# Single scores of two key tiles copied by VectorE, and one exponential for both

## The chip, the cores and the metric

The kernel runs on one core of a Trainium2 chip. A core has engines that work side by side, each through its own queue of instructions in order: TensorE (PE, with its weight loads shown as PEld), VectorE (DVE), ScalarE (ACT), GpSimd (POOL), and SyncE (SP), which issues most DMAs. They meet through semaphores: an instruction can wait for a count that another engine raises. Matrix products are written to PSUM, eight banks of 128 partitions x 512 single-precision numbers; the other engines read them there.

The metric is the device time of one execution, in microseconds (us).

## The reference

The input x is 2048 rows of 448 numbers. Two kinds of layer alternate, attention and feed-forward, twice, with the same weights both times:

```
x = x + A(layernorm(x)); x = x + B(layernorm(x)); x = x + A(layernorm(x)); x = x + B(layernorm(x))

A: q = (x wq) in 16 heads of 28;  k = x wk, v = x wv  (one head of keys and values, shared)
   p = softmax(q k^T * 28**-0.5);  o = p v;  result = o wo
B: (silu(x w_gate) * (x w_up)) w_down        with 1792 hidden columns
```

All is single precision.

## The kernel before

**Precision.** Most products are made of three reduced-precision ones (high x high, low x high, high x low), so a score tile takes three rounds of matmuls, z = 0, 1, 2 in `step` (line 604).

**Scores.** Queries are cut into 16 groups: 4 chunks of 512 queries by 4 groups of 4 heads. For each group the 16 key tiles of 128 keys are gone through. `step(n)` makes the scores of one key tile for four heads: 4 matmuls of 32 rows a round, side by side on PE. Three heads go to a triple of PSUM banks (`three`, there are two, in turn), the fourth head, the single score (`one`), to bank 6 or 7. Two key tiles, an even and an odd step, make a pair. There are 128 pairs in a layer, 256 in the kernel.

**Exponentials.** ACT makes the exponential of the triple in one instruction of 1,536 elements a partition (line 617 in an even step, 611 in an odd one) into `pt`, which has three buffers. In an even step ACT makes the single score's exponential first, straight from PSUM (line 616). In an odd step DVE copies the single score to SBUF (`raw`, line 613), and ACT makes its exponential from there, after the triple's (line 614).

**Value product.** After an odd step, `pv(d - 1)` multiplies the probabilities of the pair before with the values (line 647): 8 matmuls, four of the even tile and four of the odd one. Values have a column of ones, so the row sums come with the product. It is written to the bank that held the even single score of the current pair, and accumulated by DVE in SBUF (line 657; line 654 copies it for the first pair of a group).

The banks of the singles change hands in this order: value product of pair d − 1 and even single score of pair d + 1 use one of banks 6 and 7 and its neighbour by turns, given by `single`. On PE the order of a pair is: even scores, odd scores, value product of the pair before.

**Around it.** When a group is finished, `post` loads its row sums (SP, line 668), and three pairs later the block in `due` runs: two checks and a reciprocal on DVE (lines 674 to 676), a store and a reload on SP (678, 679), a product and a split in high and low part on POOL (686, 139, 140). In `scores` this block comes at the end of an odd step, behind `pv` and `between`. `between` issues, once in four groups, the output projection of a finished chunk (line 587), 48 matmuls, whose results DVE adds to x (591). Pieces of the next normalisation are put behind single steps through `later` (statistics, scaling, transposes, and lines 283 and 288, which make high and low part of the transposed input). After step 1 of a layer, `maxima` (line 424 on PE, 426 to 435 on DVE) makes row maxima of the last chunk, with bank 6 for its product.

The order on each engine is as the program writes it down; nothing is rearranged (a manual schedule).

Of the kernel before, what the change touches and what calls it, by code (L numbers as in the profile page):

```python
# [8 lines left out]
F32 = mybir.dt.float32  # L9
F32R = mybir.dt.float32r  # L10
AF = mybir.ActivationFunctionType
# [4 lines left out]
P = 128  # L16
# [11 lines left out]
SCALE = DH ** -0.5  # L28
# [24 lines left out]
def forward(  # L53
# [14 lines left out]
    nc = tc.nc  # L68
# [88 lines left out]
    def weights(fc):  # L157
        fs = slice(P * fc, P * fc + P)
        r = wpool.tile([P, 4, 2, P], F32, name="wr")
        for b, src in enumerate((w_gate, w_up)):  # L160
            rows3(r[:, :, b, :], src[:, fs])
        rd = wpool.tile([P, D], F32, name="wdr")
        nc.sync.dma_start(rd, w_down[fs, :])
        h = wpool.tile([P, 4, 2, P], F32R, name="wgh", bufs=FG + 1)
        l = wpool.tile([P, 4, 2, P], F32R, name="wgl", bufs=FG + 1)
        dh = wpool.tile([P, D], F32R, name="wdh", bufs=FG + 1)
        dl = wpool.tile([P, D], F32R, name="wdl", bufs=FG + 1)
        split(h, l, r)
        split(dh, dl, rd)
        return h, l, dh, dl  # L170
# [161 lines left out]
    class Attention:  # L332
# [232 lines left out]
        def scores(self, ff):  # L565
            next(switch)
            with tc.tile_pool(name=f"at{self.layer}", bufs=1, reuse_waits="tile") as wp:
                woh = wp.tile([P, NG, D], F32R, name="woh")
                wol = wp.tile([P, NG, D], F32R, name="wol")
                on, accs, pts = {}, {}, {}  # L570
                todo, due = [], {}
                single = lambda d: banks[6 + d % 2]

                def load_wo(z):
                    r = wpool.tile([P, 4, 2, P], F32, name="wr").rearrange("p (z k) b n -> p z (k b n)", z=2)
                    nc.gpsimd.memset(r, 0.0)
                    for j in range(4):
                        nc.sync.dma_start(r[32 * j : 32 * j + DH, :, 0:D], wos[j][:, 2 * z : 2 * z + 2, :])
                    zs = slice(2 * z, 2 * z + 2)
                    split(woh[:, zs, :], wol[:, zs, :], r[:, :, 0:D])  # L580
# [14 lines left out]
                def step(n):  # L595


                    i, kt = divmod(n, NT)
                    three, one = threes[n % 2], single(n // 2 + n)
                    q, k, ks = qts[i % 2], keys[kt // 4], slice(P * (kt % 4), P * (kt % 4) + P)  # L600
                    for z, (kp, part) in enumerate(((0, 0), (1, 0), (0, 1))):
                        for j in range(4):
                            js = slice(32 * j, 32 * j + 32)
                            nc.tensor.matmul(  # L604
                                three[:, j, :] if j < 3 else one, k[js, kp, ks], q[js, part, :],
                                start=(z == 0), stop=(z == 2), tile_position=(32 * j, 0),
                            )
                    pt = wp.tile([P, 3, 512], F32, name="pt", bufs=3)
                    pt1 = wp.tile([P, 512], F32, name="pt1", bufs=3)
                    if n % 2:  # L610
                        nc.scalar.activation(pt, three, AF.Exp, scale=SCALE)  # L611
                        raw = wp.tile([P, 512], F32, name="raw")
                        nc.vector.tensor_copy(raw, one)  # L613
                        nc.scalar.activation(pt1, raw, AF.Exp, scale=SCALE)  # L614
                    else:
                        nc.scalar.activation(pt1, one, AF.Exp, scale=SCALE)  # L616
                        nc.scalar.activation(pt, three, AF.Exp, scale=SCALE)  # L617
                    pts[n] = [*(pt[:, j, :] for j in range(3)), pt1]

                def between(d):  # L620

                    i, kt = divmod(2 * d, NT)
                    free, one = threes[0], single(d + 1)
                    if full:
                        self.lent = free[:, 0, :]
                        if 6 <= kt < 14:
                            self.advance(min(NM // 4, NM * (i + 2) - self.done))
                        if kt == 14 and i + 1 < len(GR):
                            self.places[i + 1](free[:, 1, :])
                    if not todo or kt != 10:  # L630
                        return
                    c = todo.pop()
                    adds = []
                    for t in (1, 2, 3):
                        adds.append(outproj(c, t, free[:, t - 1, :]))
                    for f in adds:
                        f()
                    outproj(c, 0, one)()

                def pv(d):  # L640


                    i, kt = divmod(2 * d, NT)
                    po = single(d + 1)
                    for n in (2 * d, 2 * d + 1):
                        for j in range(4):
                            nc.tensor.matmul(  # L647
                                po[32 * j : 32 * j + 32, :], vsb[:, n % NT, :], pts[n][j],
                                start=(n == 2 * d), stop=(n > 2 * d), skip_group_check=True,
                            )  # L650
                        del pts[n]
                    if kt == 0:
                        accs[i] = halves("o2").bitcast(F32)
                        nc.vector.tensor_copy(by_tile(accs[i][:, 0, :]), in_turn(po))
                    else:
                        acc = by_tile(accs[i][:, 0, :])
                        nc.vector.tensor_tensor(acc, in_turn(po), acc, ALU.add)  # L657
                    if kt == NT - 2:
                        due[d + 3] = post(i)
# [34 lines left out]
                for c in range(3):  # L694
                    ff.X[c] = xtile(xpool) if c < 2 else None
                    fs, got = norm_steps(c, True)
                    n = NT * (4 * c + 5)
# [10 lines left out]
                for n in range(last):  # L708
                    i, kt = divmod(n, NT)
                    if kt == 0 and i + 1 < len(GR):  # L710
                        self.parts(i + 1)
                    if kt == 3 and i + 1 < len(GR) and not full:
                        self.rows(i + 1)
                    if kt == 12 and i + 2 < len(GR):
                        self.stack(i + 2)
                    if i in (2, 3) and kt == 8:
                        load_wo(i - 2)
                    if n == NT and ff.nxt:
                        ff.nxt.below(nc.sync)
                    if kt == 8 and 10 < i <= 11 + FG:  # L720
                        ff.W[i - 11] = weights(i - 11)
                    step(n)
                    if not full and n == 1:
                        self.maxima(NC - 1, (6,))
                    if n in later:
                        later.pop(n)()
                    d, odd = divmod(n, 2)
                    if odd:
                        if d:
                            pv(d - 1)  # L730
                        between(d)
                        if d in due:
                            due.pop(d)()
                pv(last // 2 - 1)
                self.lent = None
                next(switch)
# [251 lines left out]
    for c in range(1, NC):  # L988
        fs, got = norm_steps(c)
        n = 4 * c - 4  # L990
# [38 lines left out]
```

## Time and profile before

| | |
|---|---|
| median of 3 runs | 1986.07 us (1986.04 to 1986.16) |
| span of the profiled execution | 1984.8 us |
| PE busy | 1969.2 us, 99% |
| ACT busy | 1278.6 us, 64% |
| DVE busy | 812.1 us, 41% |
| POOL busy | 528.7 us, 27% |
| granted PE clock | full in all slices but those at the very end, 0.98 from 1900 us on |

The profile is of one execution; the page gives its span, from the first instruction to the last, and no other time of it. Rows of groups read: line, engine, operation, output <- input, shapes, count | busy time in all, mean duration in ns of one | idle time of the engine just before them, with what ended it. Rows of the timeline read: start (us from the span's start), duration, engine, line, operation, output <- input, and in brackets the idle time ahead of it and what ended it. Successive instructions of one engine can overlap a little, so the distance of two starts can be less than the duration. In attention, roughly 64 to 572 us and 1046 to 1555 us of the span, ACT is busiest; in feed-forward PE.

### The profile page before, as it was taken

How to read it: one execution, taken by the hardware profiler on the slowest of the kernel's cores; microseconds unless marked ns; L12 is line 12 of the kernel's file. 1: busy time of each engine (PE TensorE's matmuls, PEld its weight loads, DVE VectorE, ACT ScalarE, POOL GpSimd, SP SyncE). 2: the span in 40 equal slices, each digit the busy share in tenths (PEclk: the TensorE clock that was granted, in tenths of full speed). 3: DMA queues.
4: the chain of work that ended last, by engine and by line, in shares of the span. 5: the costliest groups of instructions: out<-in, count | busy, mean ns of one | idle time of the engine just before them, and what ended most of it. 6: DMA issues, size and time to landing. Idle time of an engine off the chain costs nothing. (4 is left out here: it accounts for less than half of the span.)

```text
span 1984.8 us, 44687 instructions
## 1 busy us (share of the span) xinstructions
PE 1969.2 (99%) x18519; PEld 1322.9 (67%) x18519; DVE 812.1 (41%) x1410; ACT 1278.6 (64%) x2140; POOL 528.7 (27%) x571
## 2 busy tenths in 40 slices
PE   9999999999999999999999999999999999999998
PEld 7544545445458999999984444454454789988887
DVE  7444543544434222322554335445454432222222
ACT  4899797997953333333349998979979433333332
POOL 4212111132213233333341221111231232233320
PEclk9999999999999999999999999999999999999999
DMA  5101020121210011100131111102111101011102
GB/s 163 55 23 31 23 51 21 32 58 28 72 33 9 24 32 32 32 24 19 51 107 35 30 31 30 44 12 61 32 55 45 31 17 30 18 31 32 32 1 76
DMA packets 93382, 77.52 MB, mean 39 GB/s; under 512 B 23510, under 2 KB 76374, under 8 KB 93174
## 3 DMA queue, kind: packets, MB, share of 16 engines
q1 hardware_dynamic: 92886, 74.16, 13.5%
q8 instruction: 146, 2.39, 0.5%
q14 instruction: 62, 0.51, 0.1%
q10 hardware_dynamic: 288, 0.46, 0.1%
HBM read 55.06 MB, written 18.74 MB: 37 GB/s over the span
## 5 line engine op out<-in xcount | busy, mean ns | idle before, releaser
L647 PE MATMUL bank<-pt,vsb 128*32 128x512 f32 x4096 | 493.3, 598 | 0.5
L604 PE MATMUL bank<-qstack,keys 32*128 32x512 f32 x1536 | 484.2, 424 | 1.7 <-DVE xres L591 1.7
L604 PE MATMUL three<-qstack,keys 32*128 32x512 f32 x4608 | 461.4, 425 | 1.5 <-DVE vt L538 1.2
L604 PEld LDWEIGHTS three<-qstack,keys 32*128 32x128 f32 x4608 | 254.2, 182 | 295.0 <-ACT pt L617 181.1
L321 PE MATMUL bank<-xh,wgh 64*128 64x512 f32 x1728 | 437.5, 389 | 0.1
L611 ACT ACTIVATE pt<-three 128x1536 f32<-128x1536 f32 x256 | 372.2, 1454 | 0.6 <-ACT pt L617 0.3
L617 ACT ACTIVATE pt<-three 128x1536 f32<-128x1536 f32 x256 | 372.0, 1453 | 0.0
L321 PE MATMUL bank<-xh,wgl 64*128 64x512 f32 x1404 | 363.0, 390 | 0.0
L321 PE MATMUL bank<-wdh,h 64*128 64x448 f32 x1792 | 330.2, 364 | 1.4 <-ACT h L889 1.0
L321 PE MATMUL bank<-xl,wgh 64*128 64x512 f32 x1296 | 328.3, 389 | 0.0
L888 DVE TENSOR_TENSOR sg<-bank,sg 128x512 f32<-128x512 f32 x112 | 77.4, 691 | 497.6 <-ACT sg L887 488.4
L647 PEld LDWEIGHTS bank<-pt,vsb 128*32 128x32 f32 x4096 | 107.1, 109 | 250.2 <-issue 152.6
L613 DVE COPY raw<-bank 128x512 f32<-128x512 f32 x256 | 177.2, 692 | 230.7 <-PE bank L604 228.5
L321 PEld LDWEIGHTS bank<-xh,wgh 64*128 64x128 f32 x1728 | 256.9, 184 | 16.7 <-issue 0.9
L798 POOL TENSOR_TENSOR xres<-stage,xres 128x448 f32<-128x448 f32 x108 | 127.7, 1203 | 499.6 <-ACT stage L797 499.6
L657 DVE TENSOR_TENSOR o<-bank,o 128x512 f32<-128x512 f32 x224 | 154.9, 691 | 241.7 <-PE bank L647 237.1
L321 PEld LDWEIGHTS bank<-wdh,h 64*128 64x128 f32 x1792 | 240.5, 184 | 15.6 <-issue 2.0
L604 PEld LDWEIGHTS bank<-qstack,keys 32*128 32x128 f32 x1536 | 243.8, 183 | 4.6 <-DVE xres L591 3.6
L328 ACT COPY seen<-bank 128x1 f32<-128x1 f32 x664 | 81.0, 163 | 238.9 <-PE bank L321 236.4
L321 PEld LDWEIGHTS bank<-xh,wgl 64*128 64x128 f32 x1404 | 212.1, 184 | 13.8
L321 PE MATMUL bank<-wdl,h 64*128 64x448 f32 x896 | 215.6, 367 | 0.0
L887 ACT ACTIVATE sg<-bank 128x512 f32<-128x512 f32 x112 | 67.3, 601 | 223.2 <-PE bank L321 214.2
(127 smaller groups left out, 2259.3 us busy)
## 6 DMA issues: line engine op xcount, KB each, us to landing
o<-rd SPq DMA_DIRECT2D x32, 256.0 KB
qraw<-qd SPq DMA_DIRECT2D x128, 56.0 KB
qd<-stage SPq DMA_DIRECT2D x30, 224.0 KB
xt<-xn SPq DMA_DIRECT2D x28, 224.0 KB
wdr<-in_B_w_down_dram SPq DMA_DIRECT2D x28, 224.0 KB
xn<-xt SPq DMA_DIRECT2D x7, 768.0 KB
wr<-in_B_w_gate_dram SPq DMA_DIRECT2D x28, 192.0 KB
wr<-in_B_w_up_dram SPq DMA_DIRECT2D x28, 192.0 KB
```

What stands on the lines that cost most here:

```text
L321: nc.tensor.matmul(po, a, b, start=start, stop=stop, skip_group_check=True)
L328: nc.scalar.copy(seen[:, i : i + 1], po[:, 0:1])
L604: nc.tensor.matmul(three[:, j, :] if j < 3 else one, k[js, kp, ks], q[js, part, :], start=(z == 0), stop=(z == 2), tile_position=(32 * j, 0),)
L611: nc.scalar.activation(pt, three, AF.Exp, scale=SCALE)
L613: nc.vector.tensor_copy(raw, one)
L617: nc.scalar.activation(pt, three, AF.Exp, scale=SCALE)
L647: nc.tensor.matmul(po[32 * j : 32 * j + 32, :], vsb[:, n % NT, :], pts[n][j], start=(n == 2 * d), stop=(n > 2 * d), skip_group_check=True,)
L657: nc.vector.tensor_tensor(acc, in_turn(po), acc, ALU.add)
L798: nc.gpsimd.tensor_tensor(r, s, r, ALU.add)
L887: nc.scalar.activation(by_tile(sg), in_turn(pg[0]), AF.Silu)
L888: nc.vector.tensor_tensor(by_tile(sg), in_turn(pg[1]), by_tile(sg), ALU.mult)
```

## The change

Both single scores of a pair are now copied by DVE, into the two halves of one `raw` buffer (three buffers, 2 x 512 each), and ACT makes the exponential of both halves in place, in one instruction of 1,024 elements, after the triples of the even and the odd step. The separate `pt1` buffers go. The value product reads the fourth head's probabilities from `raw`. On ACT a pair is then: even triple, odd triple, both singles. On DVE: even copy, odd copy, accumulate of the pair before.

The block in `due` moves: it is issued after the odd step, ahead of `pv` and `between`, instead of behind them.

```diff
@@ step(n)
                     pt = wp.tile([P, 3, 512], F32, name="pt", bufs=3)
-                    pt1 = wp.tile([P, 512], F32, name="pt1", bufs=3)
+                    if n % 2 == 0:
+                        self.raw = wp.tile([P, 2, 512], F32, name="raw", bufs=3)
+                    raw = self.raw
+                    nc.scalar.activation(pt, three, AF.Exp, scale=SCALE)
+                    nc.vector.tensor_copy(raw[:, n % 2, :], one)
                     if n % 2:
-                        nc.scalar.activation(pt, three, AF.Exp, scale=SCALE)
-                        raw = wp.tile([P, 512], F32, name="raw")
-                        nc.vector.tensor_copy(raw, one)
-                        nc.scalar.activation(pt1, raw, AF.Exp, scale=SCALE)
-                    else:
-                        nc.scalar.activation(pt1, one, AF.Exp, scale=SCALE)
-                        nc.scalar.activation(pt, three, AF.Exp, scale=SCALE)
-                    pts[n] = [*(pt[:, j, :] for j in range(3)), pt1]
+                        nc.scalar.activation(raw, raw, AF.Exp, scale=SCALE)
+                    pts[n] = [*(pt[:, j, :] for j in range(3)), raw[:, n % 2, :]]
@@ scores: the loop over steps
                     d, odd = divmod(n, 2)
                     if odd:
+                        if d in due:
+                            due.pop(d)()
                         if d:
                             pv(d - 1)
                         between(d)
-                        if d in due:
-                            due.pop(d)()
```

## The prediction

> **What bounds the kernel now.** I read the page's engine totals, then the groups of instructions, then one pair of key tiles in the timeline, engine by engine, and last the odd places: change of head group, output projection, both ends of a layer.
>
> ```profile
> PE 1969.2 (99%) x18519; PEld 1322.9 (67%) x18519; DVE 812.1 (41%) x1410; ACT 1278.6 (64%) x2140; POOL 528.7 (27%) x571
> ```
> ```profile
> L616 ACT ACTIVATE pt<-bank 128x512 f32<-128x512 f32 x256 | 151.4, 591 | 63.8 <-PE bank L604 63.6
> ```
> ```profile
> L613 DVE COPY raw<-bank 128x512 f32<-128x512 f32 x256 | 177.2, 692 | 230.7 <-PE bank L604 228.5 <-ACT pt L616 2.2
> ```
>
> PE at 99% says little, because ends of matmuls are modelled. ACT's 64% is a mean over attention and feed-forward. In attention ACT hardly ever waits: 63.8 us before the even single exponential (L616), in 8 places. One steady pair, by three engines:
>
> ```profile
> 253.18 0.59 ACT L616 ACTIVATE pt<-bank 128x512 f32<-128x512 f32 x1
> 253.66 1.46 ACT L617 ACTIVATE pt<-three 128x1536 f32<-128x1536 f32 x1
> 255.00 1.46 ACT L611 ACTIVATE pt<-three 128x1536 f32<-128x1536 f32 x1
> 256.35 0.62 ACT L614 ACTIVATE pt<-raw 128x512 f32<-128x512 f32 x1
> 256.87 0.59 ACT L616 ACTIVATE pt<-bank 128x512 f32<-128x512 f32 x1
> ```
> ```profile
> 253.83 1.92 PE L647 MATMUL bank<-pt,vsb 128*32 128x512 f32 x16
> ...
> 256.26 0.39 PE L604 MATMUL bank<-qstack,keys 32*128 32x512 f32 x1
> 256.51 0.50 PE L604 MATMUL three<-qstack,keys 32*128 32x512 f32 x3
> 256.62 0.50 PE L604 MATMUL bank<-qstack,keys 32*128 32x512 f32 x1
> ...
> 257.19 0.39 PE L604 MATMUL bank<-qstack,keys 32*128 32x512 f32 x1
> 257.52 0.64 PE L647 MATMUL bank<-pt,vsb 128*32 128x512 f32 x4
> ```
> ```profile
> 255.87 0.69 DVE L657 TENSOR_TENSOR o<-bank,o 128x512 f32<-128x512 f32 x1 [1.18 <-PE bank L647]
> 257.69 0.69 DVE L613 COPY raw<-bank 128x512 f32<-128x512 f32 x1 [1.13 <-PE bank L604]
> ```
>
> ACT's four instructions start 0.48, 1.34, 1.35 and 0.52 us apart: 3.69 us a pair, back to back. PE comes round in the same 3.69 (253.83 to 257.52). So ACT sets the pace, but the question is how far behind the next limit is. Call P the start of a value product (L647), and take the distances from these rows:
>
> - The add loop. P to the start of the accumulate (L657) 2.04, its run 0.69, hand-over to the odd step's single score 0.06 (256.56 to 256.62), from there to the last single score 0.57, and to the next value product 0.33. Sum 3.69.
> - The single-score loop, not in force today. P to the last matmul of the even step's single score 2.43 (256.26). Today ACT empties that bank.
>
> Whether the last 0.33 of the add loop is PE's own or the wait for L616 is seen where a head group begins:
>
> ```profile
> 131.57 0.59 ACT L616 ACTIVATE pt<-bank 128x512 f32<-128x512 f32 x1
> 132.05 1.45 ACT L617 ACTIVATE pt<-three 128x1536 f32<-128x1536 f32 x1
> 133.43 1.45 ACT L611 ACTIVATE pt<-three 128x1536 f32<-128x1536 f32 x1
> ```
> ```profile
> 131.93 0.39 PE L604 MATMUL bank<-qstack,keys 32*128 32x512 f32 x1
> 132.26 0.64 PE L647 MATMUL bank<-pt,vsb 128*32 128x512 f32 x4
> ```
>
> There L616 was done at 132.16, 0.10 before the value product, where the usual hand-over is 0.06; PE still took 0.33 from its last score. So 0.33 is PE's own, and the add loop takes 3.68 to 3.69 whatever ACT does. The same rows give a third distance: the odd triple (L611) started 1.38 instead of 1.34 after L617, at P + 1.17. It overwrites the buffer that the first half of the value product reads (three pt buffers), so P + 1.17 is its earliest start.
>
> **The change part by part.**
>
> *ACT, steady pair.* One L616 goes (0.48 of pace), L614 becomes 1,024 wide. The trace has no 1,024-wide exponential from SBUF. From the rows, 1,024 more elements cost 1.454 − 0.59 = 0.86, so 512 cost 0.43. Spacing to the next instruction: between 0.86 (no fixed part) and 0.62 + 0.43 = 1.05 (nothing overlaps); I take 0.52 + 0.43 = 0.95, as L614 overlaps its follower today. ACT's new pace: 1.34 + 1.35 + 0.95 = 3.64, 0.05 less than now; with the bounds 3.55 to 3.74.
>
> [...]
>
> *DVE, steady pair.* A second copy of 0.692 (256 more). By the odd copy it starts 0.50 after the last matmul of its score (257.19 to 257.69) and hands over in 0.06. The value product writes into that bank, so a new loop arises: 2.43 + 0.50 + 0.69 + 0.06 = 3.68. On DVE itself there is room: accumulate to P + 2.73, even copy from P + 2.93 to 3.62, odd copy from P + 0.17 of the next pair (as now) to 0.86, idle to 2.04. Work that the kernel hangs behind an even step lies between the two copies and delays only the odd one, which has until P + 1.8.
>
> *The paired exponential.* Even probabilities now come with the odd ones. Odd triple from P + 1.17, paired one from P + 2.52, done P + 3.57, seen by PE at 3.63. It is the fourth matmul of the next value product that waits for it, at 3.69 at the earliest: not late, by 0.05.
>
> So the steady pair goes from ACT's 3.69 to the two PE–DVE loops' 3.68 to 3.69. I take 3.685: 246 ordinary pairs (128 a layer less three with an output projection and two at the ends) x −0.005 = −1.2 us. ACT's 0.05 is not collected. Bounds: 3.64 (ACT alone) and 3.73 (paired exponential with nothing overlapped, below).
>
> *Beginning of a layer.*
>
> ```profile
> 65.56 0.43 DVE L527 CAST q<-sg 112x512 fp32r<-112x512 f32 x1
> ```
> ```profile
> 66.48 1.20 PE L424 MATMUL bank<-q,kdiag 112*128 112x512 f32 x4
> ```
> ```profile
> 69.88 0.32 DVE L435 STREAM_TRANSPOSE flat<-two 128x128 f32<-128x128 f32 x1
> 70.11 0.65 DVE L613 COPY raw<-bank 128x512 f32<-128x512 f32 x1
> ```
> ```profile
> 69.50 0.64 PE L647 MATMUL bank<-pt,vsb 128*32 128x512 f32 x4
> ```
>
> The row-maximum chain (L424, then L426 to L435 on DVE) is issued after step 1. L424 writes the bank of the first even score: now DVE empties it after L527, to 65.99 + 0.69 = 66.68, so L424 starts 0.2 later. The first value product goes after even copy 1, which is queued behind L435: 70.11 + 0.2 + 0.69 + 0.06 = 71.06 instead of 69.50 today, where ACT had emptied the bank. That is +1.5 us in each layer: +3.0 (the second layer is built alike).
>
> *Output projection* (6 places): PE is the limit there, and its restart goes through the even single score.
>
> ```profile
> 215.75 0.39 PE L604 MATMUL bank<-qstack,keys 32*128 32x512 f32 x1
> ```
> ```profile
> 216.88 0.64 PE L647 MATMUL bank<-pt,vsb 128*32 128x512 f32 x4
> ```
>
> With the copy: 215.75 + 0.50 + 0.69 + 0.06 = 217.00, 0.12 later. Six times: +0.7.
>
> *End of a layer.*
>
> ```profile
> 570.28 0.62 ACT L614 ACTIVATE pt<-raw 128x512 f32<-128x512 f32 x1
> ```
> ```profile
> 570.96 0.14 PEld L647 LDWEIGHTS bank<-pt,vsb 128*32 128x32 f32 x2 [0.37 <-ACT pt L614]
> 571.93 0.19 PEld L301 LDWEIGHTS bank<-xh,wgh 128*128 128x128 f32 x1 [0.84 <-PE bank L647]
> ```
>
> The last value product had its even half done by then; only the last odd quarter waited (0.97 to the next work). Now the even half's fourth matmul waits too: exponential ends 570.28 + 1.05 = 571.33, PE goes on at 571.39, then a half product (1.92 / 2 = 0.96) and the 0.97: 573.32 instead of 571.93. Twice +1.4: +2.8.
>
> *The moved block* (row sums: checks, reciprocal, their store and reload on SP, the product on POOL). It goes ahead of the value product's accumulate in DVE order.
>
> ```profile
> 421.05 0.68 DVE L288 TENSOR_TENSOR xl<-xn,xh 128x512 fp32r<-128x512 f32 x1
> 422.32 0.69 DVE L657 TENSOR_TENSOR o<-bank,o 128x512 f32<-128x512 f32 x1 [0.60 <-PE bank L647]
> 422.93 0.16 DVE L674 TENSOR_SCALAR under<-rs 128x16 f32<-128x16 f32 x1
> ...
> 423.64 0.24 DVE L676 RECIPROCAL rs<-rs 128x16 f32<-128x16 f32 x1
> ```
> ```profile
> 256.59 2.47 SPq L668 DMA_DIRECT2D rs<-o  x4
> ...
> 264.89 0.34 SPq L678 DMA_DIRECT2D rd<-rs  x1
> 266.32 0.59 SPq L679 DMA_DIRECT2D o<-rd  x1
> ```
>
> It runs 0.95 (422.93 to 423.88). Behind the odd copy it takes P + 0.78 to 1.73, clear of the accumulate at 2.04: nothing. Its data must be there 1.9 us sooner than now: loads issued by 259.06, needed at 262.0; SP's next reload starts 1.43 after the store that it waits for, so 2.9 is enough. SP's and POOL's order stays, both start earlier. In four places a cast residue of 0.68 (L288) comes first: 0.78 + 0.60 + 0.95 = 2.33, the accumulate 0.25 late and with it the loop: +1.0.
>
> Sum: −1.2 + 3.0 + 0.7 + 2.8 + 1.0 = +6.3 us. The profiled span is 1984.8, the median of the runs 1986.07 (1.3 us lie around the span and stay). Forecast: 1992.4 us, slower by 0.3%. About 0.2%, 4 us, can be told from no change.
>
> **The rivals.**
>
> 1. *ACT's pace decides* (other side: faster). For it: no wait stands before L617, L611 or L614 today. Then 246 x −0.05 = −12.3 with the same +7.5 at the odd places: 1981.3. It decides only if the even copy starts at least 0.04 sooner than the odd one does, and the accumulate loop is as much shorter, since both stand at 3.68 to 3.69. Chance 0.15.
> 2. *The two loops have a little slack*, say 3.67, since the odd copy and the accumulate wait for one engine fewer: 246 x −0.02 = −4.9, +7.5 remain: 1988.7, no difference. Chance 0.15.
> 3. *The paired exponential is late.* If it takes 1.15 instead of 1.05 from start to hand-over, the fourth matmul waits at P + 3.73, and each pair is 0.04 longer: +9.8 + 7.5: 2003.4. It decides from 0.05 on. For it: even probabilities arrive 3 us later than now. Against: 0.62 + 0.43 comes from measured slopes. Chance 0.12.
>
> **How the numbers follow.** My case has 0.58, by itself 1989 to 1996 (steady pair ±0.015). The range reaches to rivals 1 and 3: 1981 to 2003. Slower by over 0.2%: 0.58 + 0.12 = 0.70; within: 0.15; faster: 0.15.
>
> **What would show it.** Value products 3.68 to 3.69 apart, with PE waiting for the even copy or the accumulate, and small ACT gaps ahead of the odd triple (PE the releaser); exponential of 1,024 near 1.05; first value product of a layer 1.5 later, last one 1.4 longer. Wrong: value products 3.64 apart with ACT gapless (rival 1), or PE waiting on the paired exponential (rival 3).

## The result, and the profile after

The changed kernel takes 1999.32 us (median, 1997.40 to 2001.09), beside 1986.05 us for the kernel before: a ratio of 1.0065, 95% interval 1.0051 to 1.0079. It is slower, as forecast; but the forecast was +6.3 us and the runs give +13.3. The time lies inside the stated range of 1981 to 2003 only because that range reached as far as the third rival; the prediction's own case alone had 1989 to 1996. The profiled span went from 1984.8 to 1997.4 us, +12.6.

The page of the kernel after, its span and engine totals:

```profile
span 1997.4 us, 44353 instructions
...
PE 1972.4 (99%) x18519; PEld 1304.2 (65%) x18519; DVE 985.9 (49%) x1666; ACT 1283.6 (64%) x1884; POOL 527.5 (26%) x571
```

ACT has 256 instructions fewer and 5 us more busy time, DVE 256 more and 174 us more. The groups of instructions:

```profile
L612 ACT ACTIVATE pt<-three 128x1536 f32<-128x1536 f32 x512 | 736.0, 1447 | 71.0 <-PE three L604 59.3 <-PE bank L645 9.7 <-PE bank L604 0.6
...
L613 DVE COPY raw<-bank 128x512 f32<-128x512 f32 x512 | 354.8, 694 | 90.8 <-PE bank L604 53.0 <-PE three L604 21.4 <-ACT pt L612 0.6
...
L615 ACT ACTIVATE raw<-raw 128x1024 f32<-128x1024 f32 x256 | 268.7, 1050 | 0.0
```

The paired exponential (now L615) takes 1.050 us, as estimated (1.05). In the list of waits, PE stands ahead of each value product (now L645) for the copies, where before it stood there for ACT's even single exponential (us in total, times, longest; before, then after):

```profile
PEld bank L647 <- ACT pt L616: 94.7, 254, 0.6
```
```profile
PEld bank L645 <- DVE raw L613: 116.5, 254, 1.7
```

One steady pair, from the timeline: first PE, then DVE, then ACT.

```profile
252.14 0.63 PE L645 MATMUL bank<-pt,vsb 128*32 128x512 f32 x3
...
254.57 0.39 PE L604 MATMUL bank<-qstack,keys 32*128 32x512 f32 x1
...
255.45 0.39 PE L604 MATMUL bank<-qstack,keys 32*128 32x512 f32 x1
255.85 0.63 PE L645 MATMUL bank<-pt,vsb 128*32 128x512 f32 x3
```
```profile
254.13 0.69 DVE L655 TENSOR_TENSOR o<-bank,o 128x512 f32<-128x512 f32 x1 [1.27 <-PE bank L645]
255.11 1.47 DVE L613 COPY raw<-bank 128x512 f32<-128x512 f32 x2 [0.28 <-PE three L604]
```
```profile
251.90 2.87 ACT L612 ACTIVATE pt<-three 128x1536 f32<-128x1536 f32 x2
254.66 1.05 ACT L615 ACTIVATE raw<-raw 128x1024 f32<-128x1024 f32 x1
255.61 1.44 ACT L612 ACTIVATE pt<-three 128x1536 f32<-128x1536 f32 x1
```

The value products are 3.71 apart here (252.14 to 255.85). Over all ordinary pairs (235 of them lie between 3.55 and 3.78) the mean is 3.717; in the kernel before it was 3.695 over 241. So the pair did not become shorter by 0.005, it became longer by 0.022.

The loop that sets it is the one through the even copy. P is 252.14 again: the last matmul of the even single score starts at P + 2.43 (254.57), as forecast; the copy starts 0.54 later (255.11), not 0.50; it takes 0.69, and PE goes on 0.05 after it. Sum 3.71 to 3.72. The other loop, through the accumulate, has become shorter than forecast: the accumulate (now L655) starts at P + 1.99, not 2.04, so that 1.99 + 0.69 + 0.06 + 0.57 + 0.33 gives 3.64.

The places that the forecast named at the edges of a layer came as written. Beginning of the first layer, in the timeline of all engines and then of DVE and PE:

```profile
66.09 0.50 PE L424 MATMUL bank<-q,kdiag 112*128 112x512 f32 x1 [0.21 <-DVE raw L613]
```
```profile
69.35 0.31 DVE L435 STREAM_TRANSPOSE flat<-two 128x128 f32<-128x128 f32 x1
69.58 1.25 DVE L613 COPY raw<-bank 128x512 f32<-128x512 f32 x2
```
```profile
70.29 0.63 PE L645 MATMUL bank<-pt,vsb 128*32 128x512 f32 x3 [1.23 <-DVE raw L613]
```

The first value product waits 1.23 us for the copy queued behind the row maxima. From the layer's first score to it there are 6.95 and 6.97 us in the two layers, before 5.49 and 5.41. End of the first layer:

```profile
575.09 1.05 ACT L615 ACTIVATE raw<-raw 128x1024 f32<-128x1024 f32 x1
...
576.19 0.11 PEld L645 LDWEIGHTS bank<-raw,vsb 128*32 128x32 f32 x1 [1.75 <-ACT raw L615]
...
578.02 0.19 PEld L301 LDWEIGHTS bank<-xh,wgh 128*128 128x128 f32 x1 [0.84 <-issue]
```

From the last score to the feed-forward's first weight load it takes 5.87 in both layers, before 4.49 and 4.50.

One kind of place had not been foreseen. Two pairs of the kernel after took 4.44 us. All engines, around one of them:

```profile
372.12 1.55 DVE L234 TENSOR_SCALAR sg<-xres,mv,rstd 128x448 f32<-128x448 f32 x1
372.13 1.29 POOL L684 TENSOR_TENSOR o<-o 128x512 f32<-128x512 f32 x1 [9.26 <-DMA o<-rd]
...
373.59 0.68 DVE L655 TENSOR_TENSOR o<-bank,o 128x512 f32<-128x512 f32 x1
```

A scaling of the next normalisation (L234, median 0.53) took 1.55 while POOL's product with the reciprocal row sums (L684) ran, and the accumulate stood behind it. In the kernel before, no such scaling took more than 0.92. The scaling ends 0.25 after the product does, though it is shown as starting 0.01 ahead of it. The other of the two pairs has the same: a scaling at 1361.01 that takes 1.42 and ends 0.25 after a product of 1.29.

### The profile page after: what moved, and what is told of

It reads as the page before. It is cut to its first block, busy times and chain, and to the rows that moved or that the text cites. A ratio compares the mean times of both kernels' runs of the same rounds, so it can differ in the third digit from the quotient of the medians.

```text
span 1997.4 us, 44353 instructions
## 1 busy us (share of the span) xinstructions
PE 1972.4 (99%) x18519; PEld 1304.2 (65%) x18519; DVE 985.9 (49%) x1666; ACT 1283.6 (64%) x1884; POOL 527.5 (26%) x571
## 3 DMA queue, kind: packets, MB, share of 16 engines
q1 hardware_dynamic: 92886, 74.16, 13.2%
## 5 line engine op out<-in xcount | busy, mean ns | idle before, releaser
L612 ACT ACTIVATE pt<-three 128x1536 f32<-128x1536 f32 x512 | 736.0, 1447 | 71.0 <-PE three L604 59.3
L645 PE MATMUL bank<-pt,vsb 128*32 128x512 f32 x3072 | 490.8, 598 | 8.2 <-DVE raw L613 3.5
L645 PE MATMUL bank<-raw,vsb 128*32 128x512 f32 x1024 | 487.4, 598 | 1.7 <-ACT raw L615 1.7
L604 PE MATMUL bank<-qstack,keys 32*128 32x512 f32 x1536 | 471.3, 424 | 2.4 <-DVE xres L591 1.7
L613 DVE COPY raw<-bank 128x512 f32<-128x512 f32 x512 | 354.8, 694 | 90.8 <-PE bank L604 53.0
L645 PEld LDWEIGHTS bank<-pt,vsb 128*32 128x32 f32 x3072 | 101.8, 109 | 269.6 <-issue 152.5
L615 ACT ACTIVATE raw<-raw 128x1024 f32<-128x1024 f32 x256 | 268.7, 1050 | 0.0
L655 DVE TENSOR_TENSOR o<-bank,o 128x512 f32<-128x512 f32 x224 | 154.6, 690 | 219.2 <-PE bank L645 217.9
L321 PEld LDWEIGHTS bank<-xh,wgl 64*128 64x128 f32 x1404 | 212.0, 184 | 14.7
```

The source lines that it names most:

```text
L321: nc.tensor.matmul(po, a, b, start=start, stop=stop, skip_group_check=True)
L604: nc.tensor.matmul(three[:, j, :] if j < 3 else one, k[js, kp, ks], q[js, part, :], start=(z == 0), stop=(z == 2), tile_position=(32 * j, 0),)
L613: nc.vector.tensor_copy(raw[:, n % 2, :], one)
L615: nc.scalar.activation(raw, raw, AF.Exp, scale=SCALE)
L645: nc.tensor.matmul(po[32 * j : 32 * j + 32, :], vsb[:, n % NT, :], pts[n][j], start=(n == 2 * d), stop=(n > 2 * d), skip_group_check=True,)
```

## The experiments

The question was why the steady pair is 3.717 and not 3.685, and what the rest of the 12.6 us is. Theory A: the even copy waits for two engines, for PE, whose score it copies, and for ACT, which last wrote that `raw` buffer; the second wait delays it, and it stands in the loop that sets the pair. Rivals: the copy's place in the loop costs this much with one wait too (B), or PE or ACT sets the pair and the copy only follows (C).

The trace bears on how many waits an instruction has. The line view lists, beside L613, separate semaphore instructions on DVE's queue that belong to it. Before (odd copies only), then after (both):

```profile
L613 DVE COPY raw<-bank x256: 652/692/811, 66.6 to 1549.4; 128x512 f32<-128x512 f32 x128
L613 DVEq EVENT_SEMAPHORE  x254: 21/21/21, 69.9 to 1549.3; - x127
```
```profile
L613 DVE COPY raw<-bank x512: 651/692/843, 65.3 to 1560.8; 128x512 f32<-128x512 f32 x171
L613 DVEq EVENT_SEMAPHORE  x238: 21/21/21, 76.8 to 1560.0; - x119
```

Before, nearly every odd copy had one; after, 238 for 512 copies: nearly all even copies have them (236), of the odd ones two. That such an instruction stands for a second wait is the author's reading. It goes with the program, which lets the odd copies before and the even copies after wait for PE and for ACT, and with experiment 1, where ACT's wait is taken off the even copy and none of the 512 copies has one.

The kernel after holds a test of theory A in itself. Eight ordinary pairs, the third of each layer and those behind the six output projections, have an even copy without such an instruction. One of them, DVE and then PE:

```profile
221.65 1.52 DVE L613 COPY raw<-bank 128x512 f32<-128x512 f32 x2 [0.23 <-PE bank L604]
```
```profile
221.17 0.39 PE L604 MATMUL bank<-qstack,keys 32*128 32x512 f32 x1
...
222.40 0.63 PE L645 MATMUL bank<-pt,vsb 128*32 128x512 f32 x3
```

The copy starts 0.48 after its last matmul, and the value product 3.66 after the one before (which started at 218.74). All eight start 0.46 to 0.48 after it, and their pairs take 3.65 to 3.66.

**1. The second wait taken off the even copy.** A memset of four padding columns of the next pair's buffer, behind the odd copy, takes over the wait for ACT at a time when DVE is idle.

```diff
                     pt = wp.tile([P, 3, 512], F32, name="pt", bufs=3)
+                    if n == 0:
+                        self.slot = wp.tile([P, 1028], F32, name="raw", bufs=3)
                     if n % 2 == 0:
-                        self.raw = wp.tile([P, 2, 512], F32, name="raw", bufs=3)
+                        self.raw = self.slot[:, 0:1024].rearrange("p (b n) -> p b n", b=2)
...
                     pts[n] = [*(pt[:, j, :] for j in range(3)), raw[:, n % 2, :]]
+                    if n % 2 and n + 1 < NT * len(GR):
+                        self.slot = wp.tile([P, 1028], F32, name="raw", bufs=3)
+                        nc.vector.memset(self.slot[:, 1024:1028], 0.0)
```

> The kernel after, but a tiny VectorE instruction behind the odd copy (4 columns beside the next pair's singles) takes the wait for ScalarE on the buffer, so that the even copy waits for TensorE alone. Theory A (the even copy's second wait is why it starts 0.54 us after its last matmul where the odd one needs 0.44): start 0.44 to 0.48, value products 3.64 to 3.66 apart instead of 3.716, 246 pairs, 13 to 18 us less: 1982 to 1986 us. Rival B (TensorE signals the even score late because the odd step's matmuls follow at once): start stays at 0.54, time stays at 1999 us. Rival C (ScalarE's odd triple, which waits for the value product, sets the pair): the copy starts sooner, but value products stay 3.71 apart, 1999 us.

Measured: 1984.91 us beside 1986.38 for the kernel before, ratio 0.9992 (0.9983 to 1.0002): no difference from it, and 14.4 less than the kernel after. One steady pair, PE and then DVE (the copy is L615 in this kernel, the value product L650, the memset L621, the accumulate L660):

```profile
254.02 0.63 PE L650 MATMUL bank<-pt,vsb 128*32 128x512 f32 x3
...
256.45 0.39 PE L604 MATMUL bank<-qstack,keys 32*128 32x512 f32 x1
...
257.67 0.63 PE L650 MATMUL bank<-pt,vsb 128*32 128x512 f32 x3
```
```profile
256.01 0.69 DVE L660 TENSOR_TENSOR o<-bank,o 128x512 f32<-128x512 f32 x1 [1.20 <-PE bank L650]
256.92 0.69 DVE L615 COPY raw<-bank 128x512 f32<-128x512 f32 x1 [0.22 <-PE bank L604]
257.76 0.69 DVE L615 COPY raw<-bank 128x512 f32<-128x512 f32 x1 [0.15 <-PE bank L604]
258.40 0.06 DVE L621 MEMSET raw<- 128x4 f32 x1
```

The even copy now starts 0.47 after its last matmul (256.45 to 256.92), 0.07 sooner, and the pair is 3.65 (254.02 to 257.67; mean 3.655 over 232), 0.062 shorter by the means: 246 pairs make 15 us, against 14.4 between the medians of this kernel and the kernel after. An added instruction made the kernel faster, because it takes a wait from one in the loop; its 512 copies have no semaphore instructions of their own any more, where the kernel after has 238. Theory A stands, B and C fall. ACT runs through in this kernel:

```profile
252.89 1.05 ACT L617 ACTIVATE raw<-raw 128x1024 f32<-128x1024 f32 x1
253.84 2.81 ACT L614 ACTIVATE pt<-three 128x1536 f32<-128x1536 f32 x2
256.54 1.05 ACT L617 ACTIVATE raw<-raw 128x1024 f32<-128x1024 f32 x1
```

Its starts, 252.89 and 256.54, are the same 3.65 apart, 0.95 for the paired exponential and 2.70 for two triples: the pace 3.64 of the forecast. Copy loop (2.43 + 0.47 + 0.69 + 0.06) and ACT now stand at the same length, so by these sums nothing more is to be had from the copy alone.

**2. The edges of a layer.** The first two pairs and the last pair of each layer take the form of the kernel before (ACT makes the even single score's exponential from PSUM), the others stay.

```diff
-                    nc.scalar.activation(pt, three, AF.Exp, scale=SCALE)
-                    nc.vector.tensor_copy(raw[:, n % 2, :], one)
-                    if n % 2:
+                    if n in (0, 2, NT * len(GR) - 2):
+                        nc.scalar.activation(raw[:, 0, :], one, AF.Exp, scale=SCALE)
+                        nc.scalar.activation(pt, three, AF.Exp, scale=SCALE)
+                    else:
+                        nc.scalar.activation(pt, three, AF.Exp, scale=SCALE)
+                        nc.vector.tensor_copy(raw[:, n % 2, :], one)
+                    if n in (1, 3, NT * len(GR) - 1):
+                        nc.scalar.activation(raw[:, 1, :], raw[:, 1, :], AF.Exp, scale=SCALE)
+                    elif n % 2:
                         nc.scalar.activation(raw, raw, AF.Exp, scale=SCALE)
```

> The kernel after, with the first two pairs and the last pair of each layer as before (ScalarE takes the even single score from PSUM, the odd one on its own). Theory (the first value product waits for a copy behind the row-maximum chain, the last one for the paired exponential): first scores to first value product back from 6.95 to 5.5 us, last scores to feed-forward from 5.87 to 4.5, in both layers: 5.7 us less, 1993.6 us; the middle unchanged at 3.72 a pair. Rival (both are hidden or come back later): within 1 us of 1999.3.

Measured: 1993.86 us, ratio 1.0035 (1.0021 to 1.0050), with the steady pair at 3.716, the same as in the kernel after. First score to first value product 5.45 and 5.39: all of the 3.0 came back. Last score to feed-forward 4.98 and 4.98: 1.8 of the 2.75 came back. Half a microsecond a layer stays, and the trace shows where. In the last pair ACT first has the paired exponential of the pair before (at 570.61, for 1.05), and only then the even single score's (L613, at 571.55), for which the value product next to the last waits:

```profile
572.19 0.63 PE L651 MATMUL bank<-pt,vsb 128*32 128x512 f32 x3 [0.42 <-ACT raw L613]
```

**3 and 4. The moved block.** Once it is put back in the changed kernel (behind `pv` and `between`), once it is moved forward in the kernel before, with nothing else changed.

```diff
                     if odd:
-                        if d in due:
-                            due.pop(d)()
                         if d:
                             pv(d - 1)
                         between(d)
+                        if d in due:
+                            due.pop(d)()
```

> The kernel after, with the block in due put back behind the value product and between. Theory (the moved block costs only where another VectorE instruction comes first): the pairs of 3.84 to 3.86 and perhaps those of 4.44 go, 1 to 2 us less: 1997 to 1998 us. Rival (the move is the main cost of the change): 6 us less or more, 1993 us or below. Rival (the move protects the even copy, which otherwise queues behind the block): 32 blocks of 0.95 us behind the accumulate push the even copy by 0.7 each, 20 us more, 2019 us.

> The kernel before, with the block in due moved ahead of the value product, and nothing else. Theory (the block fits between the odd copy and the accumulate): 1986 to 1987 us, no difference. Rival (the move by itself costs): 1990 us or more.

Measured: put back in the changed kernel, 2014.01 us, ratio 1.0137 (1.0120 to 1.0154); moved forward in the kernel before, 1987.55, ratio 1.0007 (0.9997 to 1.0017), no difference. The first was expected at 1997 to 1998 and missed; what came is its last rival, the move protecting the even copy, at 14.7 us in place of 20. Put back, thirty pairs take 4.15 or 4.16 instead of 3.72. One of them, DVE and then PE:

```profile
106.85 0.69 DVE L655 TENSOR_TENSOR o<-bank,o 128x512 f32<-128x512 f32 x1 [1.27 <-PE bank L645]
107.46 0.17 DVE L672 TENSOR_SCALAR under<-rs 128x16 f32<-128x16 f32 x1
...
108.17 0.25 DVE L674 RECIPROCAL rs<-rs 128x16 f32<-128x16 f32 x1
108.33 1.22 DVE L613 COPY raw<-bank 128x512 f32<-128x512 f32 x2
```
```profile
104.86 0.63 PE L645 MATMUL bank<-pt,vsb 128*32 128x512 f32 x3
...
109.01 0.63 PE L645 MATMUL bank<-pt,vsb 128*32 128x512 f32 x3 [0.45 <-DVE raw L613]
```

The block fills DVE from 107.46 to 108.42, where the even copy should have started, at 107.84 (0.54 after its last matmul, at 107.30). It starts 0.49 late and the value product 0.44 late; thirty times 0.44 are 13.2 of the 14.7 us. In the kernel before, no even copy is there to be held up, and the move is worth nothing. So the move belongs to the change: without it the changed kernel is slower than the kernel before by 28 us and not by 13.

**5. Experiments 1 and 2 together.**

> Both edits together: the tiny VectorE instruction that takes the buffer's wait, and the first two and the last pair of each layer as before. Theory (steady pair and ends are independent, each worth what it was alone): 14.4 + 5.5 us less than the kernel after, 1979.4 us, that is 6 to 7 us less than the kernel before (0.3%). Rival (with the pair at 3.65 ScalarE is the bound again, and what the ends give is lost there): 1983 to 1985 us, no difference from before.

Measured: 1980.57 us, ratio 0.9969 (0.9957 to 0.9981), faster than both kernels (1979.4 was expected); pair 3.65, attention 504.8 and 504.5 us a layer, before 507.9 and 507.2.

**6 and 7. The pieces of the normalisation half a head group later**, away from the moved block: first in the changed kernel, then on top of experiment 5.

```diff
                     fs, got = norm_steps(c, True)
-                    n = NT * (4 * c + 5)
+                    n = NT * (4 * c + 5) + 8
```

> The kernel after, with the pieces of the next normalisation behind 8 steps later, so that none stands ahead of the moved block and the scaling does not meet GpSimd's product of the outputs. Theory (the two pairs of 4.44 are VectorE's scaling held up while GpSimd works; the pairs of 3.84 to 3.86 are the block behind such a piece): both kinds go, 2 x 0.72 + 6 x 0.13 = 2.2 us less, 1997.1 us, no L234 above 0.7 us on this stretch. Rival (these pairs have another cause): they stay, 1999.3 us.

> That shift with the two edits before it (the tiny instruction, and the ends as before). Theory (independent again): 2.2 us below 1980.6, 1978.4 us, 0.4% less than the kernel before. Rival (with ScalarE at its own pace of 3.65 single delays are made up): 1980 to 1981 us.

Measured: 2013.57 us (1.0136, 1.0120 to 1.0151) and 1994.92 (1.0039, 1.0026 to 1.0053); both missed. The pieces got away from the block, and into other work of POOL. Experiment 6, DVE and then POOL, in the two places:

```profile
438.60 0.69 DVE L613 COPY raw<-bank 128x512 f32<-128x512 f32 x1
439.20 2.18 DVE L288 TENSOR_TENSOR xl<-xn,xh 128x512 fp32r<-128x512 f32 x1
```
```profile
438.35 2.49 POOL L140 TENSOR_TENSOR wgl<-wr,wgh 128x1024 fp32r<-128x1024 f32 x1
```
```profile
514.87 0.51 DVE L234 TENSOR_SCALAR sg<-xres,mv,rstd 128x448 f32<-128x448 f32 x1 [4.93 <-POOL rstd L226]
515.30 0.68 DVE L655 TENSOR_TENSOR o<-bank,o 128x512 f32<-128x512 f32 x1
```

In the first, a cast residue (L288, otherwise 0.68) took 2.18 while POOL split feed-forward weights (438.35 to 440.84). The copy from PSUM beside it, in POOL's time too, took its usual 0.69. In the second, DVE waited 4.93 us for a reciprocal standard deviation that POOL had behind that splitting, with the accumulate queued behind the wait (POOL again, then PE):

```profile
509.33 2.38 POOL L140 TENSOR_TENSOR wgl<-wr,wgh 128x1024 fp32r<-128x1024 f32 x1
...
513.82 1.01 POOL L226 TENSOR_TENSOR rstd<-rstd,halfn 128x4 f32<-128x4 f32 x1
```
```profile
516.03 0.79 PE L604 MATMUL bank<-qstack,keys 32*128 32x512 f32 x1 [3.62 <-DVE o L655]
```

The value products are 8.39 us apart there, 8.20 in the other layer. PE stands for 3.62 us, and its granted clock is 0.50 from 514.26 to 521.09, so that the next pair is long too: 5.45, and 6.03 in the other layer, with the matmuls of its value product starting 0.85 apart instead of 0.43. The four long pairs are 13.2 of the 14 us to the kernel after. Experiment 7 has the same four, at 8.29, 6.01, 8.74 and 5.83.

**8 and 9. The same shift only for the first two chunks' statistics, scaling and transposes**, where POOL has no weights to split: in the changed kernel, and on top of experiment 5.

```diff
                     for kt, f in enumerate(fs):
-                        later[n + kt] = f
+                        later[n + kt + (8 if c < 2 else 0)] = f
```

> The kernel after, with only the statistics, scaling and transposes of the first two chunks 8 steps later; their high and low parts and the third chunk stay. GpSimd has no weights to split at these places, as it had in the run before. Theory (VectorE's scaling is held up while GpSimd has an instruction with two SBUF inputs in work): the two pairs of 4.44 and those of 3.84 go, 1.4 to 1.8 us less, 1997.5 us, longest L234 on these rows under 0.7 us. Rival (other cause): unchanged, 1999.3 us, pairs of 4.4 elsewhere.

> The same smaller shift on top of the tiny instruction and the ends as before (1980.6 us). Theory: its pairs of 4.86 and 4.34 go, 1.9 us less, 1978.7 us. Rival: 1980 to 1981 us, no difference that can be told.

Measured: 1998.23 us (1.0060, 1.0044 to 1.0075), expected 1997.5. The two pairs of 4.44 are gone, and the longest scaling is now 0.74, from 1.55 (under 0.7 was expected). Ten pairs of 3.82 to 3.91 are still there, against what was expected. The step is too small against the spread of the runs to be told from the kernel after by the times. On top of experiment 5: 1979.59 us (0.9966, 0.9954 to 0.9978), the lowest of all, where 1978.7 was expected, and not to be told from experiment 5.

## Why the prediction was right in sign and short in size

Terms of its sum, beside what the traces give. The steady term is 246 times the change of the mean pair; the ends are the differences above; the output projection is the sum of six pairs' lengths, 86.2 less 85.8; the odd pairs are what single pairs take above the ordinary ones, after less before. The measured rows add up to 12.8 and not 12.6, because the steady pairs and the end of a layer overlap by 0.1 in each layer.

| term | forecast | measured |
|---|---|---|
| steady pairs | −1.2 | +5.5 |
| beginning of a layer, two | +3.0 | +3.0 |
| end of a layer, two | +2.8 | +2.75 |
| output projection, six | +0.7 | +0.4 |
| moved block and other odd pairs | +1.0 | +2.1 |
| outside attention | 0 | −1.0 |
| span | +6.3 | +12.6 |

**Steady pair: the step that failed is "by the odd copy it starts 0.50 after the last matmul".** The even copy took 0.54, so that the single-score loop is 3.72 and not 3.68. The row taken was of an instruction with two waits, and the even copy has two as well, so the number was near; but this hand-over stands in the loop that sets 246 pairs, and the term came out 6.7 us too low. After the change the odd copy has one wait, and starts 0.43 after its last matmul (255.45 to 255.88, the second of the group of two that starts at 255.11), where the kernel before took 0.50 with two. Experiment 1 has the even copy at 0.47 with one, 0.54 with two. Both pairs of numbers give 0.07 for the second wait. That the even copy is 0.04 behind the odd one in either case is not explained.

Not every semaphore instruction costs this. The accumulate, before and then after:

```profile
L657 DVEq EVENT_SEMAPHORE  x224: 21/1789/1987, 73.4 to 1552.0; - x112
```
```profile
L655 DVEq EVENT_SEMAPHORE  x162: 21/21/21, 74.0 to 1563.5; - x162
```

Before, the semaphore instruction itself was held until PE had finished (1.79 us in the median), and the accumulate started at P + 2.05 in the median. After, most accumulates still have one, but it is passed at once, some 1.9 us ahead of them; they start at P + 1.99, the same as the 62 that have none. So the 0.05 to 0.07 us are seen where the separate instruction comes right ahead of the one that works (it starts 0.06 before the copy in the median, and before the accumulate it ended 0.05 ahead), and not where it was passed 1.9 us earlier.

**ACT's pace 3.64** was right, and so was the reason why it isn't collected: the loops. Which loop was wrong: both had been put at 3.68 to 3.69, and they parted to 3.64 (accumulate, which no longer waits for ACT) and 3.72 (even copy). ACT's pace fell from 3.69 to 3.65 at most, 246 times 0.04, about 10 us, and only in experiment 1.

**Rivals.** The first, ACT's pace deciding, is nearly what experiment 1 brings about, and nearly by the condition that the prediction set: the even copy starts 0.03 sooner than the 0.50 of the sum (0.04 was asked for), the accumulate 0.05. With the edges mended too it gave 1980.57 us. The second was half right: the odd copy and the accumulate, each with a wait fewer, did gain 0.05 to 0.07; it overlooked that the even copy, new in the loop, brings a second wait. The third did not happen: the paired exponential takes 1.050, and in steady pairs no wait of PE for it appears.

**Beginning and end** were right to 0.1 us, in place, releaser and size. **Output projection** was in the right direction and too large: four of the six places went from 14.25–14.27 to 14.29–14.31, 0.04 each and not 0.12. The even copy has no semaphore instruction there and starts 0.43 after its last matmul, where the sum had 0.50. The rest of the +0.4 is a longer form of 14.45 to 14.49, at two places now and at one before; its cause is open.

**Moved block.** Where a cast residue stands before it, pairs of 3.84 to 3.86 appear, at the four places of the forecast, at +0.13 each and not +0.25: the accumulate starts at P + 2.27 (forecast 2.33) and is shown with 0.63 instead of 0.69, so it ends 0.21 late, and 0.08 of that is taken up between the two loops. A meeting of POOL's product with DVE's scaling was not in the sum at all; there are two, at 0.72 each. That the move makes them is not shown: with the block put back (experiment 3) one scaling also takes 1.55, so it seems to hang on where the two happen to fall. That the move is free was true of the block by itself (experiment 4); the prediction did not ask what would happen without it, which is 13 us more (experiment 3).

The fall outside attention (−1.0 us in span) and three pairs of 4.07 to 4.08 were not explained; in those three the even copy starts 0.42 us after its semaphore instruction where 0.06 is usual.

## What to carry to other kernels

When a loop of two engines sets the pace, count the engines that each instruction in it waits for, see which of the waits ends last, and let an instruction in an idle stretch take the extra one: here a memset of 0.06 us took 0.07 out of a loop that runs 246 times. When an operation moves to another engine, look at what stands ahead of the new copy in that engine's order and who waits behind it, at the first and last turn of a loop too, where nothing covers it. When work moves in time, read what DVE and POOL then do at the same moment.

## What the runs showed of the hardware that was not expected

- Three DVE instructions started 0.05 to 0.07 us later where a separate semaphore instruction came right ahead of them (0.43 against 0.50 for the odd copy, 0.47 against 0.54 for the even one, P + 1.99 against P + 2.05 for the accumulate), although that instruction is shown with 0.02 us ahead of the copies. One that the accumulate had passed 1.9 us before cost nothing: P + 1.99 with it and without.
- Some DVE operations from SBUF to SBUF ended only after POOL's product or split of SBUF tiles had: a 128x448 scaling took 1.55 instead of 0.53 beside a POOL product of 1.29, a 128x512 subtraction 2.18 instead of 0.68 beside a split of 2.49. They ended 0.25 and 0.55 us after it. Others took their usual time: in the kernel after, a transpose (L239) 1.05 beside a POOL split of 1.28, a maximum (L428) 0.69 beside one of 1.29. A DVE copy from PSUM was not held either (0.69 inside those 2.49 us).
- While PE stood for 3.62 us, its granted clock fell to 0.50 and stayed there for 6.8 us (experiment 6; matmuls of a value product 0.85 apart then, 0.43 otherwise).
